# The first load of a DMA-fed decode kernel, issued as 16 rows and then the other 112

## The chip, the core and the metric

The kernel runs on one core of a Trainium2 chip. The metric is the device time of one execution in microseconds; the kernel before takes 1300.84 us (median of three runs).

## The reference

One decode step of a transformer block with a cache, for two sequences. All arithmetic is in float32.

```python
B, Sq, D = 2, 1, 512
H, Sk, Dh = 32, 8192, 128          # heads, cached positions, head size

def _A_ref(x, k_cache, v_cache, wq, wo):
    q = (x @ wq).reshape(B, Sq, H, Dh).transpose(0, 2, 1, 3)
    scores = jnp.einsum("bhqd,bhkd->bhqk", q, k_cache) * (Dh ** -0.5)
    p = softmax(scores, axis=-1)
    o = jnp.einsum("bhqk,bhkd->bhqd", p, v_cache)
    return o.transpose(0, 2, 1, 3).reshape(B, Sq, H * Dh) @ wo

def _B_ref(x, w1, b1, w2, b2):     # D -> F = 1792 -> D
    r = maximum(jnp.einsum("bsd,df->bsf", x, w1) + b1, 0)
    return jnp.einsum("bsf,fd->bsd", r * r, w2) + b2

h = x + _A_ref(layernorm(x), k_cache, v_cache, wq, wo)
out = h + _B_ref(layernorm(h), w1, b1, w2, b2)
```

The two caches hold 2 x 32 x 8192 x 128 floats each, 512 MiB together; every byte of them is read once.

## The kernel before

The SBUF holds one large tensor, `ring`, of three places of 16,384 floats (64 KB) in each of the 128 partitions. `place(u)` is one of them; `slot(i)` is place `i % 3`. A pair of a sequence and a head (there are 64) fills one place: the first half of each row holds keys, the second half values. Such a load, `slot(i) <- kvd[i]`, is 128 rows of 64 KB, 8 MB in all. The query weights `wqd` have the same shape and go to place 2 first.

All loads are issued on SP's queue. A small helper, the class `Line`, records the operations of the start and of the end of the program, works out who must wait for whom, and gives every load a semaphore of its own; its operations appear in the profile under the helper's lines (a load is L136, a matmul L139, a DVE reduction L165, an activation L143). A load in `Line` also waits for the eighth load before it in the same recorded part (`AHEAD = 8`); the first part records three loads.

The start: SP issues `wqd` into place 2, the two rows of x (`xd`) twice into the tile `xr`, at partitions 0 and 32, and then the caches of pairs 0 and 1 into places 0 and 1 (L218). DVE and ACT normalize x as soon as the second copy in `xr` has landed, PE turns it into `xn`, and PE then multiplies it with the weights in place 2 (`WQ`), which gives the queries in `QT`. When the projection has read place 2, SP issues the cache of pair 2 into it (L307).

The loop: 63 pairs, three in each turn. For each pair, PE waits for its load, computes the scores (32 matmuls, L345), DVE takes the maximum, ACT the exponentials with their sum, and DVE multiplies with the values and sums up (four operations, L363). Then the place is free, and SP, which waits for that (L318 is the helper of such waits), issues the load three pairs on (L329). The projection, the second half of the block and the last pair follow in a written-out end, whose loads (`wod`, `w1d`, `w2d`, the last cache in pieces) go into places that come free. At the end SP stores the result: 98 rows of 128 floats, `out <- res`.

Of the kernel before, what the change touches and what calls it, by code (L numbers as in the profile page):

```python
# [10 lines left out]
P = 128  # L11
# [162 lines left out]
def attention_block_kernel(nc, xd, kvd, wqd, wod, w1d, w2d, out):  # L174
    def sb(name, *shape):
        return nc.alloc_sbuf_tensor(name, [P, *shape], F32).ap()

    written = nc.alloc_semaphore("written")
    line = Line(nc)
# [12 lines left out]
    def place(u):  # L192
        return ring[:, u * ROW : (u + 1) * ROW]
# [16 lines left out]


    xr = sb("xr", D)
    line.load(place(2), wqd)
    line.memset(xr, 0.0)
    for at in (0, 32):
        line.load(xr[at : at + B], xd)
# [71 lines left out]
    for k in range(2):  # L288
        for d in range(DB):
            for j in range(NQ):  # L290
                n = k * NQ + j
# [4 lines left out]
    for k in range(2):  # L296
        for m in range(NQ):
            at = k * BLK + m * DH
# [189 lines left out]
    at = 0  # L488
# [3 lines left out]
    at = 0  # L492
# [49 lines left out]
    for e in range(NH + 1):  # L542
        at = 32 * min(e, NH - 1)
# [31 lines left out]
    for m in range(FB):  # L575
# [3 lines left out]
        if m == W2_PIECES[0] - 1:  # L579
            for j in range(NQ):  # L580
                at = o[32 * j : 32 * j + B, :]
# [41 lines left out]
```

## Time and profile before

| | |
|---|---|
| median of three runs | 1300.84 us (1300.77 to 1301.26) |
| the profiled execution | 1301.16 us, span 1299.8 us |
| DMA queue of SP | 561.08 MB, 99.7% of 16 engines' span |
| mean rate over the span | 432 GB/s |
| DVE, PE, ACT busy | 57%, 32%, 11% of the span |
| granted TensorE clock, mean | 0.634 |

Times in rows of the profile are microseconds from the start of the span unless marked otherwise. "SPq" is the queue of SP, and the duration of such a row is that of issuing, not of the transfer. Rows of DMA issues end with the median time from issue to landing. The DMA share is the mean busy share of the core's 16 DMA engines.

### The profile page before, as it was taken

How to read it: one execution, taken by the hardware profiler on the slowest of the kernel's cores; microseconds unless marked ns; L12 is line 12 of the kernel's file. 1: busy time of each engine (PE TensorE's matmuls, PEld its weight loads, DVE VectorE, ACT ScalarE, POOL GpSimd, SP SyncE). 2: the span in 40 equal slices, each digit the busy share in tenths (PEclk: the TensorE clock that was granted, in tenths of full speed). 3: DMA queues.
4: the chain of work that ended last, by engine and by line, in shares of the span. 5: the costliest groups of instructions: out<-in, count | busy, mean ns of one | idle time of the engine just before them, and what ended most of it. 6: DMA issues, size and time to landing. Idle time of an engine off the chain costs nothing. (4 is left out here: it accounts for less than half of the span.)

```text
span 1299.8 us, 6711 instructions
## 1 busy us (share of the span) xinstructions
PE 422.4 (32%) x2418; PEld 113.7 (9%) x2418; DVE 742.9 (57%) x709; ACT 143.7 (11%) x149; POOL 0.7 (0%) x6
## 2 busy tenths in 40 slices
PE   1423233223323323313313323322323332331347
PEld 0100000000000000000000000000000000000012
DVE  1355655655665564665665565665566565657474
ACT  1110010111011011011011011011101011101111
POOL 0000000000000000000000000000000000000000
PEclk9766566666566566656566556656656656666678
DMA  9999999999999999999999999999999999999998
GB/s 420 420 450 419 450 421 442 430 426 446 422 448 421 450 422 442 430 430 442 422 450 421 448 424 448 422 450 421 436 436 421 450 422 448 424 448 422 450 412 371
DMA packets 11069, 561.16 MB, mean 432 GB/s; under 512 B 1234, under 2 KB 1332, under 8 KB 1720
## 3 DMA queue, kind: packets, MB, share of 16 engines
q1 hardware_dynamic: 11064, 561.08, 99.7%
q8 instruction: 4, 0.07, 0.0%
q14 instruction: 1, 0.01, 0.0%
HBM read 561.03 MB, written 0.05 MB: 432 GB/s over the span
## 5 line engine op out<-in xcount | busy, mean ns | idle before, releaser
L345 PE MATMUL s<-ring,q 128*32 128x512 f32 x2016 | 376.1, 914 | 831.2 <-PEq L318 831.2
L363 DVE SCALAR_TENSOR_TENSOR ring<-ring,s 128x2048 f32<-128x2048 f32 x252 | 561.5, 2285 | 143.1 <-DVEq L318 143.1
L351 DVE TENSOR_REDUCE st<-s 128x1 f32<-128x2048 f32 x63 | 144.4, 2292 | 341.9 <-DVEq L318 341.9
L358 ACT ACTIVATE s<-s,st 128x2048 f32<-128x2048 f32 x63 | 122.3, 1942 | 1083.4 <-ACTq L318 1083.4
L345 PEld LDWEIGHTS s<-ring,q 128*32 128x32 f32 x2016 | 94.5, 159 | 1112.0 <-issue 1112.0
L363 DVE DVE_READ_ACCUMULATOR ring<-ring,s 128x1 f32 x252 | 21.0, 83 | 0.0
L367 DVE TENSOR_SCALAR ALL<-st 128x6 f32 x63 | 10.8, 172 | 15.2 <-DVEq L318 15.2
L165 DVE TENSOR_REDUCE sx<-xr 2x1 f32<-2x512 f32 x1 | 0.7, 676 | 21.2 <-DMA xr<-in_xd 21.2
L358 ACT ACTIVATION_READ_ACCUMULATOR s<-s,st 128x1 f32 x63 | 12.1, 193 | 0.0
L139 PE MATMUL s<-ring,OT 128*2 128x512 f32 (+1 forms) x70 | 10.8, 689 | 3.6 <-DMA ring<-in_wod 3.0
L139 PE MATMUL s<-ident,xr 128*128 128x4 f32 x8 | 1.9, 356 | 26.0 <-DVE xr L157 26.0
L139 PE MATMUL s<-ring,xn 128*2 128x512 f32 x64 | 9.2, 742 | 0.3 <-DVE xn L150 0.3
L161 DVE SCALAR_TENSOR_TENSOR ring<-ring,s 128x2048 f32<-128x2048 f32 x3 | 6.8, 2283 | 1.4 <-DMA ring<-in_kvd 1.4
L139 PE MATMUL s<-ring,QR 128*32 128x512 f32 x32 | 5.3, 825 | 4.6 <-DMA ring<-in_kvd 4.6
L157 DVE TENSOR_SCALAR QT<-s 128x64 f32<-128x64 f32 x1 | 0.2, 225 | 10.3 <-PE s L139 10.3
L139 PE MATMUL s<-ring,xc 128*2 128x448 f32 (+1 forms) x34 | 5.6, 725 | 0.3 <-DVE xc L153 0.3
L143 ACT ACT_TABLE_LOAD x4 | 5.1, 1283 | 0.8 <-PEq L615 0.7
L354 DVE TENSOR_SCALAR q<-QT 128x96 f32 x21 | 5.1, 243 | 0.0
L139 PE MATMUL s<-ALL,pick 128*128 128x62 f32 (+1 forms) x16 | 3.4, 352 | 5.1 <-PEq L464 4.5
L139 PE MATMUL s<-ring,a 128*2 128x128 f32 x112 | 3.6, 272 | 2.5 <-DMA ring<-in_w2d 1.8
L139 PEld LDWEIGHTS s<-ident,xr 128*128 128x128 f32 x8 | 1.8, 327 | 26.0 <-DVE xr L157 26.0
L150 DVE COPY res<-s 128x128 f32<-128x128 f32 x1 | 0.3, 292 | 5.9 <-PE s L139 5.9
(86 smaller groups left out, 50.9 us busy)
## 6 DMA issues: line engine op xcount, KB each, us to landing
ring<-in_kvd SPq DMA_DIRECT2D x1, 4096.0 KB, 28.3
ring<-in_wod SPq DMA_DIRECT2D x1, 4096.0 KB, 18.1
ring<-in_kvd SPq DMA_DIRECT2D x1, 3584.0 KB, 26.3
ring<-in_w1d SPq DMA_DIRECT2D x2, 1792.0 KB, 24.8
ring<-in_wod SPq DMA_DIRECT2D x1, 2560.0 KB, 31.8
ring<-in_w2d SPq DMA_DIRECT2D x2, 1280.0 KB, 30.5
ring<-in_wod SPq DMA_DIRECT2D x1, 1568.0 KB, 18.2
ring<-in_kvd SPq DMA_DIRECT2D x63, 37.3
```

The lines of the kernel that those rows point to most:

```text
L139: self.op("pe", lambda e: e.matmul(out, lhsT, rhs, start=start, stop=stop), [lhsT, rhs], [out])
L143: self.op("act", lambda e: e.activation(out, in_, func, bias=bias, scale=scale, accum_out=accum_out), [in_, *more], [out] + ([] if accum_o ...
L150: self.op("dve", lambda e: e.tensor_copy(out, in_), [in_], [out])
L157: self.op("dve", lambda e: e.tensor_scalar(out, in_, by, None, op0=ALU.mult), [in_, *more], [out])
L161: self.op("dve", lambda e: e.scalar_tensor_tensor(out, a, by, b, op0=op0, op1=op1, accum_out=accum_out), [a, b, *more], [out] + ([] if acc ...
L165: self.op("dve", lambda e: e.tensor_reduce(out, in_, axis=AX.X, op=op, negate=negate), [in_], [out])
L345: made = pe.matmul(bk[n][32 * j : 32 * j + 32, :], q3[:, u, :], keys(u)[:, j, n * BLK : (n + 1) * BLK], start=True, stop=True)
L351: dve.tensor_reduce(nm, s, axis=AX.X, op=ALU.max, negate=True).then_inc(m_full, 1)
L354: dve.tensor_scalar(q3, nxt[:, :, None].to_broadcast([P, SLOTS, 32]), 1.0, None, op0=ALU.mult)
L358: act.activation(s, s, AF.Exp, bias=nm, scale=1.0, accum_out=ls).then_inc(e_full, 1)
L363: made = dve.scalar_tensor_tensor(v, v, 1.0, s, op0=ALU.mult, op1=ALU.mult, accum_out=st3[:, u, 2 + e : 3 + e])
L367: dve.tensor_scalar(all3[:, bass.ds(r, 1), u], st3[:, u : u + 1], 1.0, None, op0=ALU.mult).then_inc(kv_free, 1)
```

## The change

The first load, 128 rows of `wqd` into place 2, becomes two loads into the same place: rows 0 to 15 (1 MB), and then rows 16 to 127 (7 MB). Each has a semaphore of its own, and the first matmul of the projection waits for both. Everything behind them on SP's queue keeps its order, and the lines from there on move by one.

```diff
     xr = sb("xr", D)
-    line.load(place(2), wqd)
+    for at, n in ((0, 16), (16, P - 16)):
+        line.load(place(2)[at : at + n], wqd[at : at + n])
     line.memset(xr, 0.0)
     for at in (0, 32):
         line.load(xr[at : at + B], xd)
```

## The prediction

> **What bounds the kernel now.** I read the page first: the DMA row of the 40 slices, the queues and the packet count, then the chain that ended last.
>
> ```profile
> DMA  9999999999999999999999999999999999999998
> DMA packets 11069, 561.16 MB, mean 432 GB/s; under 512 B 1234, under 2 KB 1332, under 8 KB 1720
> q1 hardware_dynamic: 11064, 561.08, 99.7%
> ```
>
> The DMA engines are busy in every slice; the one queue of SP takes 99.7% of sixteen engines' span. In the chain of waits, in order of time, the last stretch is two landings and a short tail:
>
> ```profile
> 1243.05 26.25 DMA ring<-in_kvd
> 1269.31 0.02 issue
> 1269.33 27.51 DMA ring<-in_w2d
> 1296.84 0.04 issue
> 1296.88 1.10 PE s L139 x32
> 1297.98 0.02 issue
> 1298.00 0.29 DVE res L150
> ```
>
> So the end comes some 3 us after the last transfer (1299.8 - 1296.84). The question is whether the queue ever runs dry, for only then could a late first load be made up. The timeline of the start, with the queue's issues and their users:
>
> ```profile
> 0.75 0.40 SPq L136 DMA_DIRECT2D ring<-in_wqd  x1
> 1.43 0.62 SPq L136 DMA_DIRECT2D xr<-in_xd  x2
> 22.80 0.68 DVE L165 TENSOR_REDUCE sx<-xr 2x1 f32<-2x512 f32 x1 [21.24 <-DMA xr<-in_xd]
> 28.19 2.74 PE L139 MATMUL s<-ring,xn 128*2 128x512 f32 x12 [0.33 <-DVE xn L150]
> 37.48 0.33 SPq L307 DMA_DIRECT2D ring<-in_kvd  x1
> 42.22 5.34 PE L345 MATMUL s<-ring,q 128*32 128x512 f32 x32 [2.94 <-PEq L318]
> 62.02 21.27 SPq L329 DMA_DIRECT2D ring<-in_kvd  x2
> ```
>
> And the rate, by windows (columns: stretch, its length, busy time of PE, PEld, DVE, ACT and POOL, granted clock, DMA share, GB/s; a packet counts whole where it starts):
>
> ```profile
> 100.00:1200.00 1100.00, 342.78 (x1824) 85.71 (x1824) 651.80 (x590) 117.34 (x114) 0.00 (x0) 0.61 1.00 434
> ```
>
> 434 GB/s over 16 engines is 27.1 GB/s each, at a share of 1.00. A full load is 128 rows of 16,384 floats, 65,536 bytes a row, so an engine takes 65,536 / 27.1 = 2.42 us a row, and a load takes 8 rows an engine = 19.35 us. From the start at 1.8 us the three first loads (wqd, kvd 0, kvd 1) keep the queue busy to about 1.8 + 0.6 + 3 x 19.35 = 60.5 us; kvd 2 is issued at 37.48, 23 us before that. The first reload is issued at 62.02, when kvd 2 still has 60.5 + 19.35 - 62.0 = 18 us to run. From there each slot comes free one load's time after the other, and this row holds the same picture for all of them:
>
> ```profile
> ring<-in_kvd SPq DMA_DIRECT2D x63, 37.3
> ```
>
> 37.3 us from issue to landing is 19.35 us of its own and 18 us behind the load before it. The queue never runs dry, with 18 us in hand. So whatever the engines lose in the first load is lost at the end too, one for one; and since every load gives each engine a fixed set of rows, it is the engine that lost most that sets the end.
>
> **How a load is shared out.** The packet count tells it. The ring takes 76 loads of 128 rows (63 as above, 12 tail pieces, 1 wqd); three smaller DMAs remain:
>
> ```profile
> ring<-in_kvd SPq DMA_DIRECT2D x1, 4096.0 KB, 28.3
> ...
> ring<-in_w2d SPq DMA_DIRECT2D x1, 256.0 KB, 22.1
> out<-res SPq DMA_DIRECT2D x1, 49.0 KB
> xr<-in_xd SPq DMA_DIRECT2D x2, 4.0 KB
> ring<-in_wqd SPq DMA_DIRECT2D x1, 22.0
> ```
>
> 1234 packets lie under 512 B, and nothing here moves such data: they are completions, one for each engine that takes part. 76 x 16 = 1216, and 18 are left for 98, 2 and 2 rows: 14 + 2 + 2, the largest divisor up to 16. By that, 16 rows go to 16 engines, one row each, and 112 rows to 16, seven each. No engine gets more rows than before, and the packet count rises by 16 only.
>
> **The change, part by part.** *One more issue on SP.* The wqd row above is 0.40 us, so the 112 rows and everything behind them on SP (both xd loads, kvd 0 and 1) are issued some 0.4 us later. The cover is the first row, which runs for about 3 us, and after that the queue; without it the price would be 0.4. I take 0. *One more completion* an engine: nothing against 2.42 us. *One more wait*: the projection on PE now needs both pieces. Behind it on PE are only the projection and the scores, and DVE, ACT and SP wait for these; it costs as much as the last piece is late, with the 18 us above as cover. I take 0. No compute instruction is added, removed or moved, on POOL neither.
>
> *An earlier start.* The windows of the start show when rows begin:
>
> ```profile
> 0.00:1.80 1.80, 0.00 (x0) 0.00 (x0) 0.64 (x4) 1.06 (x1) 0.70 (x6) 1.00 0.23 73
> 1.80:2.00 0.20, 0.00 (x0) 0.00 (x0) 0.00 (x0) 0.20 (x1) 0.00 (x0) 1.00 6.95 2294
> 2.00:2.50 0.50, 0.00 (x0) 0.00 (x0) 0.00 (x0) 0.49 (x2) 0.00 (x0) 1.00 2.28 786
> 2.50:3.00 0.50, 0.00 (x0) 0.00 (x0) 0.00 (x0) 0.50 (x2) 0.00 (x0) 1.00 0.30 131
> 3.00:4.80 1.80, 0.00 (x0) 0.00 (x0) 0.00 (x0) 1.43 (x2) 0.00 (x0) 1.00 0.00 0
> 4.80:5.70 0.90, 0.00 (x0) 0.00 (x0) 0.00 (x0) 0.00 (x0) 0.00 (x0) 1.00 2.69 1165
> ```
>
> GB/s times length over 65.5 KB counts the rows that begin: 2, 7, 6 and 1, all sixteen before 3.0 us, and the second sixteen between 4.8 and 5.7 (1165 x 0.9 = 1048 KB). The late starters thus made good most of it. What a shorter first issue can win is the spread of the second rows, 0 to 0.9 us; I take 0.
>
> *Where the rows land.* This is the term that decides. In the load of 128 rows each engine works at 27.1 GB/s whatever the others do. Now sixteen engines write at once into sixteen partitions that lie together. If neighbouring partitions share a way in, and that way carries about what one engine brings (27.1 GB/s), g engines on one way take g times as long. The rows show no such transfer, so bounds: g = 1 (own ways) costs nothing, g = 16 (one way for all) costs 15 x 2.42 = 36.3 us. I take the middle of 1, 2, 4, 8, 16: g = 4, **3 x 2.42 = 7.3 us**. It is no row's number; its nearest relation is that 128 partitions serve 16 engines, 8 to each, so that 16 adjoining ones have room for two full shares (g = 8), or four halves (g = 4).
>
> [...]
>
> Then the 112 rows, seven to an engine. If they are dealt in blocks, engines stand seven partitions apart, and now and then two meet on one way. The nearest row is the store at the end, 98 rows of 512 B, also seven rows to each of 14 engines:
>
> ```profile
> 1299.10:1299.50 0.40, 0.00 (x0) 0.00 (x0) 0.00 (x0) 0.00 (x0) 0.00 (x0) 1.00 0.48 126
> ```
>
> 0.48 x 16 x 0.40 = 3.07 us for 98 rows is some 31 ns a row, against 512 / 27.1 = 18.9 ns: a factor of 1.65 at most, part of it a packet's own overhead. Seven rows are 16.9 us; the factor 1 costs 0, 1.65 costs 11.0, two engines on each way all along 16.9. The worst engine counts, not the mean, so I take 1.5: **8.5 us**.
>
> Sum: 0 + 0 + 7.3 + 8.5 = **+15.8 us**. The profiled execution took 1301.16, its span and 1.36 around it; that gives 1317.0, and on the median of 1300.84, 0.3 lower, **1316.6**, 1.2% slower. Within the forecast, g = 4 with factors from 1.25 to 1.8 gives +11.5 to +20.8. An engine whose seven rows meet nobody loses 7.3, the worst 15.8; the 8.5 us between them are less than the 18 in hand, so the fast ones don't run dry either, and no second loss follows.
>
> **The rivals.** *No shared way: nothing changes.* Each engine writes as fast anywhere; the split costs 0 and may win up to 0.9 us: 1299.9 to 1301.2, not slower. For it speaks that all sixteen engines hold 27.1 GB/s each for 1100 us beside each other; against it that they never wrote to adjoining partitions then, if the load of 128 is dealt to keep them apart. It decides where the 112 rows meet nobody and g is below 2.1 (1.1 x 2.42 = 2.6 us, the 0.2% below). [...]
>
> *Only the small piece collides.* If the 112 rows are dealt so that engines stay apart, only 7.3 stays: 1308.1. The 31 ns of the store, near a bare row plus overhead, speaks for it; that blocks of seven cannot line up with groups of four or eight speaks against.
>
> *The 112 rows are dealt one by one round the engines.* Then sixteen adjoining rows are under way at each of eight steps: 8 x 7.3 = +58 us, 1358.9. The store speaks against it: at g = 4 its rows would take nearer 75 than 31 ns.
>
> *A gain past 0.2%.* It would need 2.6 us (0.2% of 1300.84, about what a measurement can tell here), while the start holds 0.9 and the other engines' time hangs on the queue. I see no mechanism.
>
> **How the numbers follow.** Forecast 0.61; only the small piece 0.14; dealt round 0.08; no shared way 0.15; gain 0.02. Slower by over 0.2%: 0.61 + 0.14 + 0.08 = 0.83; within 0.2%: 0.15; faster: 0.02. The range leaves out the dealing round and the gain (0.10) and the ends of the forecast: from 1300.2 to 1322. The likeliest case alone: 1312 to 1322.
>
> **What would show it.** If right, the windows of the changed kernel show the sixteen first rows before 3 us, the second sixteen at 4.8 + 7.3 = 12 us or later, no row beginning between, and kvd 2 issued near 37.48 + 16 = 53 us; from 100 us on again 434 GB/s, and the same three-us tail. If the second rows begin near 5 us, the shared way is refuted; if they begin near 12 and kvd 2 goes out near 45, the 112 rows met nobody; if kvd 2 goes out after 90, they were dealt round. A DMA share under 1.00 between 100 and 1200 us would show that the queue ran dry, which I exclude.

## The result, and the profile after

| | before | after |
|---|---|---|
| median | 1300.84 us | 1321.11 us (1320.58 to 1321.8, five runs) |
| profiled execution, span | 1301.16, 1299.8 us | 1321.29, 1320.0 us |
| DMA queue of SP, share of 16 engines | 99.7% | 99.7% |
| mean rate over the span | 432 GB/s | 425 GB/s |

The ratio is 1.0154 (95% interval 1.0143 to 1.0166): 20.3 us slower. The range of the prediction (1300.2 to 1322.0) holds it near its upper end; the predicted time was 1316.6. Of the eight blocks of 16 rows below, one of two executions moved 387 GB/s between 100 and 1200 us, where before, after and the six other kernels read in that stretch move 434 or 435, and its time (1507.7 us) is left out.

The page of after, the DMA rows of the 40 slices (33 us each) and the count:

```profile
DMA  9999999999999999999999999999999999999998
GB/s 218 358 435 443 425 435 443 425 435 443 425 435 443 425 435 443 425 435 443 425 435 443 425 435 441 427 435 439 427 437 439 425 439 439 423 441 439 423 430 370
DMA packets 11085, 561.16 MB, mean 425 GB/s; under 512 B 1250, under 2 KB 1348, under 8 KB 1736
```

The same row of before:

```profile
GB/s 420 420 450 419 450 421 442 430 426 446 422 448 421 450 422 442 430 430 442 422 450 421 448 424 448 422 450 421 436 436 421 450 422 448 424 448 422 450 412 371
```

The share of busy engines is as full as before. The rate is not: 218 and 358 GB/s in the first two slices, where every slice of before has 412 or more but the last. A share of 9 says that the engines hold work, not that they move it. The packets are 16 more, all of them under 512 B (1250 against 1234): the one further set of completions, 16 engines for 16 rows and 16 for 112, as foreseen.

Windows show the rows one after the other; a window that holds the start of one row of each engine was cut for each step. 16 rows are 1048.6 KB, so the mean time of a row is 1049 x share / (GB/s). A share above 1 is an effect of short windows: a row counts whole in the window where it starts. First before, then after:

```profile
0.00:3.00 3.00, 0.00 (x0) 0.00 (x0) 0.64 (x4) 2.25 (x3) 0.70 (x6) 1.00 1.03 350
```

```profile
0.00:3.00 3.00, 0.00 (x0) 0.00 (x0) 0.64 (x4) 2.25 (x3) 0.70 (x6) 1.00 2.84 350
8.50:12.00 3.50, 0.00 (x0) 0.00 (x0) 0.00 (x0) 0.00 (x0) 0.00 (x0) 1.00 1.62 300
15.00:17.00 2.00, 0.00 (x0) 0.00 (x0) 0.00 (x0) 0.00 (x0) 0.00 (x0) 1.00 2.35 524
20.00:22.00 2.00, 0.00 (x0) 0.00 (x0) 0.00 (x0) 0.00 (x0) 0.00 (x0) 1.00 1.61 524
23.00:26.50 3.50, 0.00 (x0) 0.00 (x0) 0.00 (x0) 0.00 (x0) 0.00 (x0) 1.00 1.07 300
27.00:30.00 3.00, 0.00 (x0) 0.00 (x0) 0.00 (x0) 0.00 (x0) 0.00 (x0) 1.00 1.49 350
31.00:34.50 3.50, 0.00 (x0) 0.00 (x0) 0.00 (x0) 0.00 (x0) 0.00 (x0) 1.00 1.34 300
35.50:39.50 4.00, 0.00 (x0) 0.00 (x0) 0.00 (x0) 0.00 (x0) 0.00 (x0) 1.00 1.13 262
40.00:44.00 4.00, 0.00 (x0) 0.00 (x0) 1.37 (x3) 0.00 (x0) 0.00 (x0) 1.00 0.81 264
100.00:1200.00 1100.00, 341.59 (x1824) 85.38 (x1824) 650.17 (x590) 117.34 (x114) 0.00 (x0) 0.61 1.00 434
```

The first row takes 8.5 us (before 3.1), the seven rows of the second piece 5.7, 4.7, 3.2, 3.7, 4.5, 4.7 and 4.5 (before 2.42 each), the first row of the next load 3.2. The losses are 5.4, then 31.0 - 16.9 = 14.1, then 0.8: together 20.3 us, the whole difference. From 100 us on the rate is 434 GB/s at a share of 1.00, as before. Nothing is lost after the start, and nothing is made up. The issues and users in the timeline:

```profile
0.75 0.86 SPq L136 DMA_DIRECT2D ring<-in_wqd  x2
42.56 0.68 DVE L165 TENSOR_REDUCE sx<-xr 2x1 f32<-2x512 f32 x1 [41.00 <-DMA xr<-in_xd]
57.45 0.33 SPq L308 DMA_DIRECT2D ring<-in_kvd  x1
```

The chain that ended last is the same, 20.1 us later (in_w2d until 1316.96 in place of 1296.84), and so is the way from issue to landing of the 63 loads, 37.3 us in both.

### The profile page after: what moved, and what is told of

Read it like the earlier page. It is cut to its first block, busy times and chain, and to the rows that moved or that the text cites. A ratio compares the mean times of both kernels' runs of the same rounds, so it can differ in the third digit from the quotient of the medians.

```text
span 1320.0 us, 6712 instructions
## 1 busy us (share of the span) xinstructions
PE 422.4 (32%) x2418; PEld 113.3 (9%) x2418; DVE 742.8 (56%) x709; ACT 143.7 (11%) x149; POOL 0.7 (0%) x6
## 2 busy tenths in 40 slices
DMA packets 11085, 561.16 MB, mean 425 GB/s; under 512 B 1250, under 2 KB 1348, under 8 KB 1736
## 3 DMA queue, kind: packets, MB, share of 16 engines
q1 hardware_dynamic: 11080, 561.08, 99.7%
## 6 DMA issues: line engine op xcount, KB each, us to landing
ring<-in_kvd SPq DMA_DIRECT2D x63, 37.3
```

## The experiments

Each changes the first load of the kernel before alone. The diffs show only the lines that replace it, and the comments in them are labels, which the kernels don't have. Theory A is that of the prediction: partitions that lie together share a way into the SBUF. No view shows a way; what the runs show is how long rows take. The rivals are the memory side (B), and the mere number of pieces (C).

### The same two pieces, cut by columns

```diff
-    line.load(place(2), wqd)
+    for lo, hi in ((0, ROW // 8), (ROW // 8, ROW)):
+        line.load(place(2)[:, lo:hi], wqd[:, lo:hi])
```

> The first load in two pieces as in the change, the first of 1 MB as there, but cut by columns: 128 rows of 8 KB, then 128 rows of 56 KB. Theory A (partitions that lie together share a way into the SBUF, four neighbours to a way at about one engine's rate): no loss, since all partitions take part in both pieces; 1300 to 1301.5 us. Rival B (reading rows that lie together in memory is slow): no loss either, the engines read the same rows as before. Rival C (two pieces in place of one, or the second wait of the projection, cost the time): about +20, near 1321.

Measured: 1301.05 us, ratio 1.000 (0.999 to 1.0009). A second issue, a second completion and a second wait of the projection cost nothing that can be measured (the interval is at most 1.3 us either way), and starting with 1 MB wins nothing that can be measured either. C falls.

### Eight blocks of 16 rows; every eighth row; blocks written from rows far apart

```diff
+    for at in range(0, P, 16):                              # blocks
+        line.load(place(2)[at : at + 16], wqd[at : at + 16])
...
+    for at in range(8):                                     # every eighth row
+        line.load(place(2)[at::8], wqd[at::8])
...
+    for at in range(8):                                     # blocks, read from every eighth row
+        line.load(place(2)[16 * at : 16 * at + 16], wqd[at::8])
```

> The first load as eight loads of 16 adjoining rows, one row to each of 16 engines. Theory A: every piece goes through four ways, about 9.5 us (the changed kernel's first rows ended 9.4 us after they began) where 2.42 would do: 8 x 7.1 = +57, near 1357 us. Rival B: the same, +57. Rival C: each further piece costs what the change's one further piece cost (20 us): 7 x 20 = +140, near 1441.

> The first load as eight loads of every eighth row, again one row to each of 16 engines. [...] Rival B: rows read and written are 512 KB apart, no loss, 1301. Rival C: as for eight blocks, far over 1400.

> As the eight loads of 16 adjoining rows, but each reads every eighth row of the weights, so that rows adjoin in the SBUF alone; the weights stand in other partitions, and the projection's values are not the reference's. Theory A (the SBUF side): as eight blocks, +57, near 1357. Rival B (the memory side): as every eighth row, near 1301. What C expects is the same for both.

Measured: 1355.5 us for the blocks (one execution), 1321.9 for every eighth row, 1355.2 for the blocks read from far rows. Windows of the last, and below of every eighth row:

```profile
17.00:21.00 4.00, 0.00 (x0) 0.00 (x0) 0.00 (x0) 0.00 (x0) 0.00 (x0) 1.00 2.32 262
```

```profile
6.00:8.50 2.50, 0.00 (x0) 0.00 (x0) 0.00 (x0) 0.00 (x0) 0.00 (x0) 1.00 2.05 419
```

By the same formula a row takes 9.3 us into 16 adjoining partitions (3.8 times 2.42) and 5.1 us into every eighth (2.1 times). Far rows on the memory side change nothing: B falls, and the loss sits where the rows are written. That every eighth row is slow too (5.1 us), though no two lie within eight partitions, says, by theory A, that partitions far apart can share a way. Two engines that write at the same time over one way are said to meet below.

### Halves, and 64 rows from 32, 28 and 16

```diff
+    for at in (0, 64):                                      # halves
+        line.load(place(2)[at : at + 64], wqd[at : at + 64])
...
+    for at, n in ((32, 64), (0, 32), (96, 32)):             # from 32
+    for at, n in ((28, 64), (0, 28), (92, 36)):             # from 28
+    for at, n in ((16, 64), (0, 16), (80, 48)):             # from 16
+        line.load(place(2)[at : at + n], wqd[at : at + n])
```

> The first load as rows 0 to 63 and then rows 64 to 127, four adjoining rows to each engine if they are dealt in blocks. [...] If the rows are dealt one by one round the engines: sixteen adjoining at a time, +54, near 1355.

> The first load as 64 rows from row 32, then rows 0 to 31, then rows 96 to 127. [...] 4 x 2.7 = +11, near 1312 us. Rival (any 64 adjoining rows, or any three pieces, cost the same as the halves): 5.13 a row from the first on, +21, near 1322.

> 64 rows from row 28, then 28 and 36 rows. [...]

> 64 rows from row 16, then rows 0 to 15, then rows 80 to 127. [...] Coupled engines: all sixteen near 4.7 to 5.1. Then the 16 rows at about 9.3 and 48 rows, three to an engine, at 4 to 5: +22 to +27 in all, 1323 to 1328.

Measured: halves 1322.1 us; from 32 1313.0 (1311.56 and 1314.5, the profile being of the first); from 28 1331.8; from 16 1335.6, over seven more than was expected. The run from 28 has 1260 packets under 512 B, 26 more than before, 14 and 12 for its pieces of 28 and 36 rows: these leave engines out, and its time says little of the 64 rows. In the expectation for the rows from 32, 2.7 us is the halves' 5.13 less 2.42; that it would fall on four of eight rows was the author's estimate (+11, measured +12). A window of the halves, two of the kernel from 32, two from 28, four from 16 (the last in its 48 rows):

```profile
6.00:8.00 2.00, 0.00 (x0) 0.00 (x0) 0.00 (x0) 0.00 (x0) 0.00 (x0) 1.00 2.57 524
```

```profile
7.00:8.50 1.50, 0.00 (x0) 0.00 (x0) 0.00 (x0) 0.00 (x0) 0.00 (x0) 1.00 1.61 699
16.00:18.00 2.00, 0.00 (x0) 0.00 (x0) 0.00 (x0) 0.00 (x0) 0.00 (x0) 1.00 2.56 524
```

```profile
6.50:7.40 0.90, 0.00 (x0) 0.00 (x0) 0.00 (x0) 0.00 (x0) 0.00 (x0) 1.00 0.71 146
9.50:10.50 1.00, 0.00 (x0) 0.00 (x0) 0.00 (x0) 0.00 (x0) 0.00 (x0) 1.00 2.12 918
```

```profile
6.00:8.00 2.00, 0.00 (x0) 0.00 (x0) 0.00 (x0) 0.00 (x0) 0.00 (x0) 1.00 2.54 524
8.00:11.00 3.00, 0.00 (x0) 0.00 (x0) 0.00 (x0) 0.00 (x0) 0.00 (x0) 1.00 0.00 0
11.00:13.00 2.00, 0.00 (x0) 0.00 (x0) 0.00 (x0) 0.00 (x0) 0.00 (x0) 1.00 2.55 524
37.50:41.00 3.50, 0.00 (x0) 0.00 (x0) 0.00 (x0) 0.00 (x0) 0.00 (x0) 1.00 2.38 300
```

Rows 0 to 63: 5.1 us a row. Rows 32 to 95, just as many and just as close: 2.42 us, and 5.1 us once rows 0 to 31 follow. So rows 32 to 63 are fast beside rows 64 to 95 and slow beside rows 0 to 31; by theory A, what they meet lies in rows 0 to 31. Rows 28 to 91: 146 x 0.9 / 65.5 = 2 rows begin in the first window, 5.1 us each, and 918 / 65.5 = 14 in the second, 2.42 us each. So two slow engines can leave fourteen free; which rows the two write the windows don't show. Rows 16 to 79 limit that: if moving the piece by four rows, from 32 to 28, makes two engines slow, moving it by sixteen would make eight slow, an estimate; yet all sixteen take 5.1 us (sixteen rows begin between 6 and 8 us, none until 11, and then sixteen again). The miss in that kernel's time lies in its 48 rows: 8.3 us a row where 4 to 5 had been expected, a term that no run had shown.

### How the 112 rows are dealt, and whether being first matters

```diff
+    line.load(place(2)[:16], wqd[:16])                      # every seventh row
+    for at in range(16, 23):
+        line.load(place(2)[at : at + 106 : 7], wqd[at : at + 106 : 7])
...
+    for at, n in ((0, P - 16), (P - 16, 16)):               # 112 first
+        line.load(place(2)[at : at + n], wqd[at : at + n])
```

> Rows 0 to 15 as in the changed kernel, and rows 16 to 127 as seven loads of 16 rows each, every seventh row from 16, 17, and so on. If the 112 rows of the changed kernel are dealt to the engines in blocks of seven, this gives every engine the same rows in the same order as there: the same row times (second to eighth row 5.6, 4.7, 3.2, 3.7, 4.5, 4.7, 4.5 us) and +20, near 1321. [...]

> The change turned round: 112 rows from row 0, then the last 16. If the collision depends on which partitions a piece covers and not on being first: +20, near 1321, with the row of 9.3 us as the eighth. If being first in the program matters (the slow first row of the changed kernel is a slow start): +10 to +14, near 1313.

Measured: 1321.1 us and 1321.0 us. The windows of every seventh row, at the same places as for the changed kernel, and below one of the last 16 of the kernel turned round:

```profile
0.00:3.00 3.00, 0.00 (x0) 0.00 (x0) 0.64 (x4) 2.25 (x3) 0.70 (x6) 1.00 2.88 350
8.50:12.00 3.50, 0.00 (x0) 0.00 (x0) 0.00 (x0) 0.00 (x0) 0.00 (x0) 1.00 1.54 300
15.00:17.00 2.00, 0.00 (x0) 0.00 (x0) 0.00 (x0) 0.00 (x0) 0.00 (x0) 1.00 2.38 524
20.00:22.00 2.00, 0.00 (x0) 0.00 (x0) 0.00 (x0) 0.00 (x0) 0.00 (x0) 1.00 1.62 524
23.00:26.50 3.50, 0.00 (x0) 0.00 (x0) 0.00 (x0) 0.00 (x0) 0.00 (x0) 1.00 1.08 300
27.00:30.00 3.00, 0.00 (x0) 0.00 (x0) 0.00 (x0) 0.00 (x0) 0.00 (x0) 1.00 1.51 350
```

```profile
31.00:36.00 5.00, 0.00 (x0) 0.00 (x0) 0.00 (x0) 0.00 (x0) 0.00 (x0) 1.00 1.52 197
```

Step by step these are the row times of the change (8.6, 5.4, 4.8, 3.2, 3.8, 4.5). So the 112 rows are dealt in blocks of seven: at each step the sixteen rows under way lie seven apart. Every eighth row, above, is in the same way what a load of 128 rows would have under way if it were dealt in blocks of eight. That took 5.1 us a row, and the load of 128 rows takes 2.42, so it is dealt in some other way, in which no row is slow. This is what a cut by rows loses (1.0154) and a cut by columns keeps (1.000).

Turned round, the kernel takes the same time. The 16 rows cost about the same at the end of the load as at its start (8.1 us there, less than the 9.3 expected, and 8.5 here); being first or last makes no difference that shows.

### A second limit, and what it is not

From row 28, two slow engines left fourteen at 2.42 us. In the 112 rows of the change it is otherwise: in five of the seven steps the sixteen rows take 4.5 to 5.7 us on the mean, and where sixteen begin between 15 and 17 us (524 x 2 / 65.5), no engine begins its next before 20. Two more kernels put the rows in other places:

```diff
+    for at in range(11, 18):                                # every seventh row from 11
+        line.load(place(2)[at : at + 106 : 7], wqd[at : at + 106 : 7])
+    for at, n in ((0, 11), (123, 5)):
+        line.load(place(2)[at : at + n], wqd[at : at + n])
...
+    for at, n, lo in ((24, 64, 0), (20, 64, HALF), (0, 24, 0), (88, 40, 0), (0, 20, HALF), (84, 44, HALF)):
+        line.load(place(2)[at : at + n, lo : lo + HALF], wqd[at : at + n, lo : lo + HALF])
```

> Every seventh row, 16 at a time, from row 11, 12 and so on to 17, then the 16 rows left. [...] Only row times are read; the last two loads use 11 and 5 engines.

> Two half loads (32 KB a row, 1.21 us where nobody meets): 64 rows from row 24, then 64 rows from row 20, then what is left. [...] Only row times are read.

Measured, one time each: 1329.6 and 1345.6 us, which say little, since pieces of 11, 5, 20, 24, 40 and 44 rows by the same count leave engines out, as those of 28 and 36 rows do. The windows of the first (first row; second row), and of the second kernel (second and third row from 24; a row of the piece from 20):

```profile
0.00:3.00 3.00, 0.00 (x0) 0.00 (x0) 0.64 (x4) 2.25 (x3) 0.70 (x6) 1.00 1.07 350
5.00:7.50 2.50, 0.00 (x0) 0.00 (x0) 0.00 (x0) 0.00 (x0) 0.00 (x0) 1.00 1.67 419
```

```profile
3.00:5.20 2.20, 0.00 (x0) 0.00 (x0) 0.00 (x0) 1.43 (x2) 0.00 (x0) 1.00 1.18 238
5.60:8.20 2.60, 0.00 (x0) 0.00 (x0) 0.00 (x0) 0.00 (x0) 0.00 (x0) 1.00 1.01 202
10.50:13.30 2.80, 0.00 (x0) 0.00 (x0) 0.00 (x0) 0.00 (x0) 0.00 (x0) 1.00 0.98 187
```

Sixteen rows, every seventh from 11: 3.2 us for the first row, as before the change (3.1). So sixteen rows seven apart are not slow as such. The next sixteen, one partition on, take 4.2 us on the mean of all. Half rows from 24 take 2.6 us (524 x share / (GB/s), since a row is half as long), from 20 2.75, on the mean of all sixteen; at the pace of free engines they would take 1.21. With two more slow engines for every four rows that the piece moves, as from 32 to 28, four would be slow from 24 and six from 20; at half of 5.1 us for these and 1.21 for the others the means would be 1.5 and 1.7 us, an estimate. So two slow engines can leave the others free, while from 24, 20 and 16 all sixteen fall to about the pace of the slow. The first half rests on the rows from 28 alone. In the change the two fastest steps took 3.2 and 3.7 us on the mean, and fourteen engines at 2.42 with two at 5.1 would give 2.8; there the steps of the engines overlap (fourteen rows of one step begin between 23 and 25 us, the last two between 25.5 and 26.5). Why all sixteen slow down, these runs don't show.

## Why the prediction was right, and by which steps

*The bound and the one-for-one loss* held: the queue never ran dry, 434 GB/s from 100 us on, 37.3 us from issue to landing, and the tail after the last landing as it was. The losses read row by row in the first load add up to the whole difference.

*The costs put at nothing* held: the cut by columns has the same two issues, completions and waits and stays at 1.000. The early start, for which 0 to 0.9 us was allowed, is too small for its interval (up to 1.3 us either way): no gain shows, and none of that size is excluded.

*The shared way* fits the row times (9.3 us into sixteen adjoining partitions, 2.42 in rows 32 to 95), though no view shows the way itself. The factor 4, a guess in the middle of 1 to 16 with no row behind it, measured 3.8; by that reasoning it is luck that it came so near. The term of 7.3 us was still too large: the first row takes 3.1 us anyway and took 8.5, a loss of 5.4.

*The 112 rows* are the term that was mis-sized: 8.5 us by the factor 1.5, measured 14.1 (a factor of 1.83), and 0.8 more in the first row of the next load. The store at the end, rows of 512 B seven to an engine, had been read as an upper bound of 1.65 on what neighbours in blocks of seven cost; it is none for rows of 64 KB. The prediction also took collisions for a matter of the engines that meet, with the worst engine setting the end. In fact not the worst alone was slow: in five of the seven steps the mean of all sixteen is 4.5 to 5.7 us.

*The sum* was therefore right in part by luck. Of its terms 7.3 was 1.9 too large, 8.5 was 5.6 too small, and 0.8 was not foreseen; the measured factor of 1.83 lies just above the 1.8 at which the forecast ended, and with 7.3 kept it would have led just out of the range.

*The rivals.* No shared way, with every place as fast as any other, is refuted by 64 rows from 32 (2.42 us) against 64 rows from 0 (5.1). Only the small piece collides: refuted by the seven windows. Dealt one by one round the engines: refuted by every seventh row, which repeats the change step by step; its price, +58, is about what the eight blocks cost (+54.4). The signs named ahead: the second rows begin between 8.5 and 12 us, with the 16 rows' term smaller than forecast, and kvd 2 goes out at 57.45 rather than 53 us, 4 us late like the whole.

## What to carry to other kernels

Cut a load that feeds all 128 partitions by columns, not by rows: two pieces by columns cost nothing (1.000), two by rows 20 to 21 us here, and turning their order round did not mend it. A full busy share of the DMA engines doesn't mean full rate (a share of 9 stood beside 218 GB/s here); read GB/s beside it, above all at the start. In a kernel bound by its queue from end to end, a loss in the first load comes out at the end undiminished, as the 20.3 us did here, while none of these cuts won anything.

## What the runs showed of the hardware that was not expected

- Rows 32 to 95 load at full rate (2.42 us a row of 64 KB), rows 0 to 63 at half of it (5.1 us): of two 64-row pieces it is the place that decides.
- The load of 128 rows is not dealt in blocks of eight: its rows take 2.42 us, and every eighth row, which such blocks would have under way, takes 5.1 us.
- In rows 28 to 91 two engines took 5.1 us a row and left fourteen at 2.42 us. In other pieces the mean of all sixteen is slow: 4.5 to 5.7 us a row in five of the seven steps of the change, 5.1 us from 16, 2.6 us a half row from 24. The cause is open.
